# The first weight piece in an attention + squared-ReLU MLP kernel: its two exponent activations issued later on ScalarE, its three rounding instructions moved from the first pair of heads to the second

## The chip, the cores and the metric

The kernel runs on one core of a Trainium2 chip. The metric is the device time of one execution in microseconds (us). The kernel before has a median of 878.74 us in 4 runs (878.18 to 879.36).

## The reference

The reference is a hashed attention followed by a two-layer MLP. Cut to what matters:

```python
# attention: q, k, v are (4, 8, 768, 64) float32, proj is (64, 6)
q_bits = (einsum('bhsd,dk->bhsk', q, proj) > 0)      # k_bits the same from k
mask   = bucket(q_bits)[:, :, :, None] == bucket(k_bits)[:, :, None, :]
scores = where(mask, scale * q @ k.T, -1e9)
attn   = softmax(scores);  o = attn @ v
# MLP: x is o as (3072, 512); w_in (512, 2048) and w_out (2048, 512) are float64
h = x @ w_in;  g = maximum(h, 0) ** 2;  out = (g @ w_out).astype(float32)
```

The weights `w_in` and `w_out` come as float64, 8 bytes an element. The chip's engines work in float32 here, so the kernel rounds each weight to float32 itself, out of the two 32-bit halves of the float64.

## The kernel before, in words

The work has two stages. The first, up to about 331 us of the profiled span, is the attention. It goes over `NP` = 16 pairs of heads, `pr` = 0 to 15. The second is the MLP, in four chunks of 1024 tokens, with products cut by Strassen-like sums (lines 712 and 931 are its matmuls, lines 505 to 535 part of its sums).

**One pair of heads.** A pair has six key tiles `kt` = 0 to 5 of 128 keys each. Everything here is written out by hand in the loop over `pr`; each engine runs its instructions in the order of the program.

- `score(pr, kt)` (line 396) makes the scores of one key tile for all 768 queries of both heads, in two chunks: 512 queries (both heads together 128x1024) and 256 queries (128x512). Each chunk goes into a PSUM tile from `turn(...)`, a pool of three. After each chunk ScalarE (ACT) takes the exponential out of PSUM into one of four SBUF buffers (line 413). A fourth chunk can only be begun when the exponential of the chunk three before it has been read out of its PSUM tile.
- `add_up(pr, kt)` (lines 423 and 428) adds the exponentials on VectorE (DVE), and `attend(pr, kt)` (line 438) multiplies them with the values on TensorE (PE), into the one PSUM tile `xo`. `score` of two key tiles and `attend` of two others alternate.
- `features(pr + 1, w)` (line 333) transposes the queries and keys of the next pair on DVE. `hash_bits` (line 346) multiplies them with `proj` on PE, `signs` (line 356) takes eight sign activations on ACT, and `weigh` (line 382) scales the keys' bits with one activation.
- `finish(pr - 1)` runs inside pair `pr`, after `score(pr, 1)`: the next pair's hash, then the sums (`tot`, line 455), the last two `attend`, and `spread` (line 477), which needs the reciprocals `both` that DVE makes out of `tot` (lines 460, 462, 466). `normalize(pr - 1)` (lines 487 and 493) writes `x_t` out of `xo`. Only then is `xo` free for `attend(pr, 0)`.

In the text, "score (0,4)" is `score(0, 4)`: pair 0, key tile 4; its chunks are "first" (512 queries) and "second" (256 queries). "Pair 0" is the first pair, "pair 1" the second.

**The weights beside it.** There are 32 pieces of weight (128x512 elements), two in each pair: `a` = 2 pr and `b` = 2 pr + 1. Four steps make a piece:

- `load_weight(i)` (line 130) loads it on SyncE's (SP's) DMA queue into one of three buffers `raw`.
- `part_weight(i)` is two DVE instructions (lines 143 and 147) which take the exponent (`power`) and the fraction (`top`) out of it.
- `place_power(i)` is two ACT activations (line 160, a Relu into 8-bit `small`, and line 161, a Copy back into `power`), which shift the exponent's bias and put it where float32 has it.
- `round_weight(i)` is three DVE instructions (lines 171, 176 and 179). It needs `place_power(i)`, frees the `raw` buffer, and leaves the piece in `ins` (for `w_in`). For piece 0 it issues no DMA.

In each pair, piece `a` is parted before `score(pr, 2)`, its power placed after `score(pr, 3)`, and it is rounded after `add_up(pr, 3)`. Piece `b` is parted there, its power is placed after `score(pr, 5)`, and it is rounded in the next pair, behind `features`, as `round_weight(b - 2)`.

Pair 0 differs from the others in one thing that matters here: the eight `signs` for pair 1 are issued between `score(0, 2)` and `score(0, 3)`, and `weigh(1)` after `score(0, 5)`.

Of the kernel before, what the change touches and what calls it, by code (L numbers as in the profile page):

```python
# [34 lines left out]
def kernel(  # L35
# [68 lines left out]
    def turn(name):  # L104

        return ps_s.tile([P, 2, 512], FP32, name=name, tag="turn")
# [11 lines left out]
    def goal(i):  # L118
        if i < 2 * NIN:
            return ins[i // NIN][:, i % NIN // 2, i % 2]  # L120
        return p_t.tile([P, DM], FP32, name="out_piece", bufs=3)

    def load_weight(i):
        src, r, c = pieces[i]
        if src.dtype != U64:
            goals[i] = goal(i)
            nc.sync.dma_start(out=goals[i], in_=src[r:r + P, c:c + PIECE])
            return
        raw = p_w.tile([P, PIECE, 2], U32, name="raw", bufs=3)
        nc.sync.dma_start(  # L130
            out=raw.rearrange("p f w -> p (f w)"),
            in_=src.bitcast(U32)[r:r + P, 2 * c:2 * (c + PIECE)],
        )
        raws[i] = raw
# [18 lines left out]
    def place_power(i):  # L153


        if i not in parts:
            return
        power = parts[i][0]
        small = p_w.tile([P, PIECE], U8, name="small")
        nc.scalar.activation(out=small, in_=power, func=ACTF.Relu, bias=excess)  # L160
        nc.scalar.activation(out=power, in_=small, func=ACTF.Copy, scale=2.0**23)

    def round_weight(i):

        raw = raws.pop(i, None)
        if raw is None:
            return keep_weight(i)
        goals[i] = goal(i)
        low, high = raw[:, :, 0], raw[:, :, 1]
        power, top = parts.pop(i)  # L170
        nc.vector.scalar_tensor_tensor(
            out=power, in0=high, scalar=0x80000000, in1=power,
            op0=ALU.bitwise_and, op1=ALU.bitwise_or,
        )
        one = top.bitcast(FP32)
        nc.vector.scalar_tensor_tensor(
            out=one, in0=low, scalar=2.0**-32, in1=top, op0=ALU.mult, op1=ALU.add,
        )
        nc.vector.scalar_tensor_tensor(
            out=goals[i], in0=one, scalar=2.0**-20, in1=power.bitcast(FP32),  # L180
            op0=ALU.mult, op1=ALU.mult,
        )
        keep_weight(i)

    def keep_weight(i):

        t = goals.pop(i)
        j, c = divmod(i, NIN)
        if j >= 2:
            nc.sync.dma_start(out=w_out_1[:, i - 2 * NIN], in_=t)  # L190
        elif c == NIN - 1:
            nf = NFT // 2
            for n, f, h in (0, 0, 0), (1, nf, 0), (2, nf, 1):
                put_factor(n, j * PIECE, ins[j][:, f:f + nf, h])
            nc.sync.dma_start(
                out=w_in_21[:, :, j * PIECE:(j + 1) * PIECE], in_=ins[j][:, 0:nf, 1]
            )
# [81 lines left out]
    def load_pair(pr):  # L279


        b, j = divmod(pr, PB)
        for src, name in ((q, "q_nat"), (k, "k_nat")):
            t = p_qk.tile([P, S], FP32, name=name)
            for g in range(4):
                h, e = divmod(g, 2)
                nc.sync.dma_start(
                    out=t[g * 32:(g + 1) * 32].rearrange("i (c d) -> i c d", d=32),
                    in_=src[b, 2 * j + h].rearrange("(c i) (e d) -> e i c d", i=32, e=2)[e],
                )  # L290
            nat[pr, name] = t
# [38 lines left out]
    def features(pr, w):  # L330

        feat[pr, w] = p_f.tile([P, S], FP32, name=f"feat{w}")
        nc.vector.transpose(out=feat[pr, w], in_=nat[pr, ("q_nat", "k_nat")[w]])
# [3 lines left out]
    def hash_bits(pr, banks, ws=(0, 1), cs=(0, 1)):  # L337


        for w in ws:  # L340
            hashed[pr, w] = banks
            for c in cs:
                g = 2 * w + c
                for h in range(2):
                    rows = slice(h * D, (h + 1) * D)
                    nc.tensor.matmul(  # L346
                        out=banks[g * NR_B:(g + 1) * NR_B, h, 0:HS], lhsT=projs[rows],
                        rhs=feat[pr, w][rows, c * HS:(c + 1) * HS], start=True, stop=True,
                    )

    def signs(pr, w):
        bits[pr, w] = t = all_bits[pr % 2][w]
        for c in range(2):
            at = slice((2 * w + c) * NR_B, (2 * w + c + 1) * NR_B)
            for h in range(2):
                nc.scalar.activation(  # L356
                    out=t[h * D:h * D + NR_B, c * HS:(c + 1) * HS], in_=hashed[pr, w][at, h, 0:HS],
                    func=ACTF.Sign, scale=HUGE, bias=lifts[at],
                )
# [19 lines left out]
    def weigh(pr):  # L379

        t = bits[pr, 1]
        nc.scalar.activation(out=t, in_=t, func=ACTF.Copy, scale=gains)
# [139 lines left out]
    def sum_in(m):  # L522

        c, n = divmod(m, 4)
        j, h = divmod(c, 2)
        t, at = ins[j], slice(h * NS, (h + 1) * NS)
        nf = NFT // 2
        a11, a12, a21, a22 = (
            t[:, f:f + nf, g, at] for g in range(2) for f in (0, nf)
        )  # L530
        s = in_sums[m] = p_t.tile([P, nf, NS], FP32, name=f"s_in{n}", bufs=2)
        if n == 0:
            nc.vector.tensor_tensor(out=s, in0=a21, in1=a22, op=ALU.add)
        else:
            minus(s, *(
                (in_sums[4 * c], a11), (a11, a21), (a12, in_sums.get(4 * c + 1))
            )[n - 1])
        put_factor((3, 4, 5, 6)[n], c * NS, s)
# [12 lines left out]
    def load_x(i):  # L551

        x = p_c.tile([P, NFT, NCH], FP32, name="x")
        nc.gpsimd.dma_start(out=x, in_=x_all[:, :, i * NCH:(i + 1) * NCH])
        xs[i] = x, [p_c.tile([P, 2, NCH // 2], FP32, name=f"t_x{n}") for n in range(3)]
# [23 lines left out]
    def finish(pr, beside=None):  # L579

        tot = turn("tot")
        if beside:
            beside()
        sum_up(pr, tot)
        if pr == NP - 1:
            sum_x(0, 2)
            sum_x(0, 3)
        for kt in (SB - 2, SB - 1):
            attend(pr, kt)
        spread(pr)  # L590

    with tc.manual_schedule():
# [21 lines left out]
        for pr in range(NP):  # L614
            a, b = 2 * pr, 2 * pr + 1
            more = pr + 1 < NP

            def prepare():

                hash_bits(pr + 1, turn("hash"))  # L620
                for w in (1, 0):
                    signs(pr + 1, w)


            if pr + 2 < NP:
                load_pair(pr + 2)
            if pr == X_0:
                load_x(0)
            if more and pr > 0:
                for w in range(2):  # L630
                    features(pr + 1, w)
            if pr > 0:
                round_weight(b - 2)
                load_weight(b)
                for m in sums.get(pr, ()):
                    sum_in(m)
            score(pr, 0)
            if pr == 0:
                first_keys(1, turn("hash"))
            score(pr, 1)  # L640
            if pr == 0:
                for w in range(2):
                    features(1, w)
            if pr > 0:
                finish(pr - 1, prepare if more else None)
            add_up(pr, 1)
            if pr > 0:
                normalize(pr - 1)


            if pr == X_0 + 1:
                for n in range(2):
                    load_unit(n)
            part_weight(a)
            score(pr, 2)
            if pr == 0:
                prepare()
            score(pr, 3)
            if more and pr > 0:
                weigh(pr + 1)  # L660
            place_power(a)
            attend(pr, 0)
            attend(pr, 1)
            for kt in (2, 3):
                add_up(pr, kt)
            if more:
                load_values(pr + 1)


            round_weight(a)  # L670
            part_weight(b)
            if more:
                load_weight(a + 2)
            score(pr, 4)
            score(pr, 5)
            if pr == 0:
                weigh(1)
            place_power(b)
            attend(pr, 2)
            attend(pr, 3)  # L680
            add_up(pr, 4)
            add_up(pr, 5)
# [801 lines left out]
```

## Time and profile before

| | us |
|---|---|
| median of 4 runs | 878.74 (878.18 to 879.36) |
| the profiled execution's own time | 878.9 |
| its span (first to last instruction) | 877.1 |
| PE busy in the span | 864.9 (99%) |
| DVE busy | 759.9 (87%) |
| ACT busy | 391.5 (45%) |
| PE busy in 20 to 40 us / 40 to 60 us | 18.53 / 20.00 |
| DVE busy in 36 to 340 us (304 us) | 290.63 |

The granted TensorE clock is 1.00 in the attention stage (0.997 as a mean over the span).

A row of the timeline reads: start in us, length in us, engine, line, operation, output <- inputs, how many instructions are merged into the row, and in brackets how long the engine had been idle before it and what it was released by. A merged row's length is that of all its instructions; instructions on one engine can overlap a little, so that the distance from start to start is shorter than the length of one.

### The profile page before, as it was taken

To read this page: it belongs to the slowest core of one execution; us is meant where nothing else is said; L and a number is where in the kernel's file an instruction comes from. 1 tells how busy PE (TensorE), PEld (TensorE's weight loads), DVE (VectorE), ACT (ScalarE), POOL (GpSimd) and SP (SyncE) were. 2 spreads that over 40 slices of the span, in tenths; PEclk is the share of its full clock that TensorE was granted. 3 is DMA by queue.
4 is the path that set the end of the run, shared out by engine and by line. 5 is a ranking of instruction groups with operands and counts; after the bars stand their busy time and mean duration, and the time that the engine had idled before them with its cause. 6 is when DMAs were issued, how large, how long until landed. Compare 5 with 4: busy or idle time off the path is not lost.

```text
span 877.1 us, 12130 instructions
## 1 busy us (share of the span) xinstructions
PE 864.9 (99%) x4340; PEld 519.2 (59%) x4340; DVE 759.9 (87%) x1099; ACT 391.5 (45%) x673; POOL 107.0 (12%) x172
## 2 busy tenths in 40 slices
PE   8999999999999999999999999999999999999996
PEld 4444444444444444444688865556888755568885
DVE  5999999999999998888679978888889788888875
ACT  6988888888888852222211123332111233321110
POOL 2000000000000000554032021111000211110002
PEclk9999999999999999999999999999999999999998
DMA  9677977898888526999788774536856744355565
GB/s 177 145 147 133 224 166 151 188 252 226 179 178 224 165 98 211 299 268 284 298 285 274 207 167 166 174 119 221 283 155 183 167 165 156 124 167 154 158 173 106
DMA packets 224132, 167.09 MB, mean 190 GB/s; under 512 B 164449, under 2 KB 181345, under 8 KB 224065
## 3 DMA queue, kind: packets, MB, share of 16 engines
q1 hardware_dynamic: 189152, 87.19, 41.0%
q0 software_dynamic: 12528, 41.30, 15.2%
q10 hardware_dynamic: 22384, 37.76, 14.1%
q8 instruction: 36, 0.59, 0.3%
q14 instruction: 32, 0.25, 0.1%
HBM read 124.52 MB, written 41.68 MB: 189 GB/s over the span
## 4 chain that ended last, share of the span: by engine, by line
PE 96%; DVE 2%; ACT 1%; DMA 1%; issue 0%; ACTq 0%; DVEq 0%
PE acc L712 40%; PE st L396 17%; PE acc L931 16%; PE xo L438 14%; PE acc L884 6%; PE hash L346 2%; PE tot L455 1%; DVE total L428 1%; DMA k_nat<-in_k_dram 1%; ACT bits L356 1%; ACT e L413 0%; PE xo L477 0%; DVE x_t L493 0%; PE tp L309 0%; DVE recs L487 0%
## 5 line engine op out<-in xcount | busy, mean ns | idle before, releaser
L413 ACT ACTIVATE e<-st 128x1024 f32<-128x1024 f32 x192 | 145.1, 810 | 44.9 <-PE st L396 41.0
L396 PE MATMUL st<-feat,feat 64*128 64x512 f32 (+1 forms) x768 | 150.4, 483 | 0.0
L438 PE MATMUL xo<-e,v_nat 128*64 128x512 f32 (+1 forms) x768 | 134.8, 492 | 0.0
L712 PE MATMUL acc<-b,leaf 128*128 128x256 f32 x600 | 133.2, 379 | 0.3 <-issue 0.3
L712 PEld LDWEIGHTS acc<-b,leaf 128*128 128x128 f32 x600 | 113.8, 190 | 16.6 <-issue 1.3
L428 DVE TENSOR_TENSOR total<-total,e 128x1536 f32<-128x1536 f32 x64 | 112.4, 1757 | 8.2 <-ACT e L413 3.6
L438 PEld LDWEIGHTS xo<-e,v_nat 128*64 128x64 f32 x768 | 51.3, 136 | 82.1 <-issue 74.3
L931 PE MATMUL acc<-t_x,w_unit 128*128 128x512 f32 x192 | 90.2, 592 | 0.0
L396 PEld LDWEIGHTS st<-feat,feat 64*128 64x128 f32 x768 | 66.0, 188 | 33.0 <-issue 23.2
L712 PE MATMUL acc<-t,leaf 128*128 128x256 f32 x336 | 76.2, 380 | 0.0
L356 ACT ACTIVATE bits<-hash,lifts 32x384 bf16<-32x384 f32 x120 | 68.6, 572 | 2.3 <-PE hash L346 0.5
L712 PEld LDWEIGHTS acc<-t,leaf 128*128 128x128 f32 x336 | 63.7, 190 | 9.1 <-DVE t L516 0.5
L796 DVE SCALAR_TENSOR_TENSOR b<-h 128x512 f32<-128x512 f32 x96 | 65.7, 691 | 3.0
L396 PE MATMUL st<-bits,bits 64*128 64x256 bf16 (+1 forms) x384 | 63.1, 325 | 1.7 <-ACT e L413 1.2
L931 PE MATMUL acc<-x,w_unit 128*128 128x512 f32 x128 | 60.1, 592 | 0.0
L712 PE MATMUL acc<-x,w_unit 128*128 128x512 f32 x128 | 56.6, 594 | 0.0
L712 PE MATMUL acc<-b_t,leaf 128*128 128x256 f32 x240 | 53.8, 379 | 0.0
L931 PEld LDWEIGHTS acc<-t_x,w_unit 128*128 128x128 f32 x192 | 36.5, 190 | 28.9 <-issue 26.8
L719 ACT COPY two<-acc 128x256 f32<-128x256 f32 (+1 forms) x29 | 12.5, 431 | 87.8 <-PE acc L712 81.5
L719 ACT COPY one<-acc 128x256 f32<-128x256 f32 (+1 forms) x29 | 12.5, 431 | 84.7 <-PE acc L712 60.9
L712 PEld LDWEIGHTS acc<-b_t,leaf 128*128 128x128 f32 x240 | 45.5, 190 | 6.2
L396 PEld LDWEIGHTS <-bits 64*128 64x128 bf16 x384 | 23.5, 93 | 42.5 <-issue 38.4
(159 smaller groups left out, 1165.9 us busy)
## 6 DMA issues: line engine op xcount, KB each, us to landing
leaf<-w_out ACTq DMA_DIRECT2D x142, 256.0 KB, 3.1
w_unit<-w_in SPq DMA_DIRECT2D x16, 640.0 KB, 4.0
raw<-in_moe_w_in_dram SPq DMA_DIRECT2D x16, 512.0 KB, 5.5
raw<-in_moe_w_out_dram SPq DMA_DIRECT2D x16, 512.0 KB, 4.3
w_unit<-w_in SPq DMA_DIRECT2D x8, 896.0 KB, 8.2
w_out<-sums POOLq DMA_DIRECT2D x16, 448.0 KB, 6.8
sum<-w_in SPq DMA_DIRECT2D x16, 448.0 KB, 4.9
v_nat<-in_v_dram SPq DMA_DIRECT2D x16, 384.0 KB, 4.3
```

The lines of the kernel that those rows point to most:

```text
L346: nc.tensor.matmul(out=banks[g * NR_B:(g + 1) * NR_B, h, 0:HS], lhsT=projs[rows], rhs=feat[pr, w][rows, c * HS:(c + 1) * HS], start=True, ...
L356: nc.scalar.activation(out=t[h * D:h * D + NR_B, c * HS:(c + 1) * HS], in_=hashed[pr, w][at, h, 0:HS], func=ACTF.Sign, scale=HUGE, bias=li ...
L396: nc.tensor.matmul(out=st[:, h, 0:hi - lo], lhsT=src[pr, 1][rows, key], rhs=src[pr, 0][rows, lo:hi], start=first, stop=not first,)
L413: nc.scalar.activation(out=e[:, :, lo:hi], in_=sts[i][:, :, 0:hi - lo], func=ACTF.Exp, scale=scale)
L428: nc.vector.tensor_tensor(out=totals[pr], in0=totals[pr], in1=weights[pr, kt][:, :, 0:S], op=ALU.add)
L438: nc.tensor.matmul(out=xo[h * D:(h + 1) * D, lo:hi], lhsT=nat[pr, "v_nat"][:, h, kt * D:(kt + 1) * D], rhs=weights[pr, kt][:, h, lo:hi], s ...
L455: nc.tensor.matmul(out=tot[g * 32:(g + 1) * 32, 0:HS], lhsT=ones, rhs=totals[pr][:, h, c * HS:(c + 1) * HS], start=True, stop=True,)
L712: nc.tensor.matmul(out=acc[to], lhsT=a(i), rhs=b(i), start=first and i == 0, stop=last and i == n - 1, skip_group_check=True,)
L719: nc.scalar.copy(out=t, in_=acc[of])
L796: nc.vector.scalar_tensor_tensor(out=out, in0=h, scalar=0.0, in1=h, op0=ALU.max, op1=ALU.mult)
L884: nc.tensor.matmul(out=out, lhsT=w[:, a], rhs=b, start=start, stop=stop, skip_group_check=True)
L931: nc.tensor.matmul(out=acc[to], lhsT=w[:, PLACE[a], f], rhs=bt[b](f), start=first and f == 0, stop=last and f == NFT // 2 - 1, skip_group_ ...
```

## The change

Three calls are moved, all of weight piece 0 (`a` in pair 0); the work stays the same.

- `place_power(0)`: two ACT activations, from after `score(0, 3)` to after `weigh(1)`, that is behind the four exponentials of `score(0, 4)` and `score(0, 5)`, and ahead of `place_power(1)`.
- `round_weight(0)`: three DVE instructions, from after `add_up(0, 3)` in pair 0 to pair 1, behind `features(2, ...)` and ahead of `round_weight(1)`.

`part_weight(0)` stays where it is. On DVE, `part_weight(1)` now follows `add_up(0, 3)` directly. In pairs 1 to 15 nothing else changes.

```diff
             if pr > 0:
+                if pr == 1:
+                    round_weight(0)
                 round_weight(b - 2)
                 load_weight(b)
...
             if more and pr > 0:
                 weigh(pr + 1)
-            place_power(a)
+            if pr > 0:
+                place_power(a)
             attend(pr, 0)
...
-            round_weight(a)
+            if pr > 0:
+                round_weight(a)
             part_weight(b)
...
             if pr == 0:
                 weigh(1)
+                place_power(0)
             place_power(b)
```

## The prediction

> **What bounds the kernel now.** I read three views: the page's chain, the same chain piece by piece in the first 42 us, then each engine's timeline there. The page, first:
>
> ```profile
> PE 96%; DVE 2%; ACT 1%; DMA 1%; issue 0%; ACTq 0%; DVEq 0%
> ```
>
> PE sets the end almost everywhere, so time can be won only where PE stands still. The waits of PE name few such places after 36 us: one of 0.4 us at 327.44, and in the MLP 0.8 and 0.3 us. The chain by pieces shows where ACT holds the end instead, in pair 0:
>
> ```profile
> 21.28 1.51 ACT e L413 x2
> 22.79 0.03 issue
> 22.82 0.73 ACT small L160
> 23.55 0.02 issue
> 23.57 0.63 ACT power L161
> 24.20 0.92 ACT e L413
> 25.12 0.04 issue
> 25.16 0.72 PE st L396 x6
> ```
>
> The two activations that the change moves are links of the chain: the exponential of score (0,4)'s first chunk stands behind them, and PE's fourth chunk, score (0,5)'s second, waits for it. PE's and DVE's rows, then ACT's:
>
> ```profile
> 25.16 0.29 PE L396 MATMUL st<-bits,bits 64*128 64x256 bf16 x2 [0.99 <-ACT e L413]
> ...
> 31.89 1.47 PE L346 MATMUL hash<-feat,projs 64*32 64x384 f32 x16
> ```
>
> ```profile
> 24.50 0.69 DVE L171 SCALAR_TENSOR_TENSOR power<-raw,power 128x512 uint32<-128x512 uint32 x1
> ...
> 30.63 0.97 DVE L333 STREAM_TRANSPOSE feat<-q_nat 128x768 f32<-128x768 f32 x1
> 31.53 0.94 DVE L333 STREAM_TRANSPOSE feat<-k_nat 128x768 f32<-128x768 f32 x1
> ...
> 38.13 1.02 DVE L493 SCALAR_TENSOR_TENSOR x_t<-xo,recs 128x768 f32<-128x768 f32 x1
> ```
>
> ```profile
> 26.87 0.95 ACT L382 ACTIVATE bits<-bits,gains 128x768 bf16<-128x768 bf16 x1
> 27.69 0.74 ACT L160 ACTIVATE small<-power,excess 128x512 uint8<-128x512 uint32 x1
> 28.46 0.63 ACT L161 ACTIVATE power<-small 128x512 uint32<-128x512 uint8 x1
> 29.85 3.13 ACT L413 ACTIVATE e<-st 128x1024 f32<-128x1024 f32 x4 [0.76 <-PE st L396]
> ```
>
> The reader is to see PE's 0.99 us gap; a hash of 1.47 us, where that of pair 2 takes 0.88 us (PE's weight loads wait 0.47 us for `feat`); and a DVE that has work without a break from 22.82 to the end of `x_t` at 39.15.
>
> **Step 1, the gap in pair 0.** Without the two activations the exponential of (0,4)'s first chunk starts at about 22.82, where line 160 did; its score is ready since 22.56. It lasts 1.02 us, to 23.84. PE begins (0,5)'s first chunk at 22.92 and is 1.08 us later (21.30 to 22.38 in the row before) at the next, 24.00: the PSUM tile is free then. So (0,5)'s second chunk goes from 25.16 to 24.00: **-1.16 us** on PE. The two `attend` behind it have had their inputs since 22.79, so score (1,0) goes from 28.56 to 27.40.
>
> **Step 2, the two activations in their new place.** ACT's distances from start to start in the timeline: first exponential 0.90, second 0.48, `weigh` 0.82, line 160 0.77, line 161 0.54. From 22.82: (0,4) takes 22.82 and 23.72; (0,5)'s first waits for its score until 24.20, its second starts at 25.10; `weigh(1)` at 25.58 (it was 26.87); then line 160 and 161 of piece 0 at 26.40 and 27.17, those of piece 1 at 27.71 and 28.48, end 29.11. (The exponent that piece 1 needs is there: on DVE its parting moves from 26.43 to 24.50.) The next exponential, of score (1,0), could have its score 1.29 us after PE starts it (28.56 to 29.85 now), at 28.69, and gets ACT at about 29.02. It is held 0.33 us. Who waits for it: PE's fourth chunk of pair 1, (1,1)'s second, which needs its end, 29.02 + 1.03 + 0.04 = 30.09; PE arrives there at 31.26 - 1.16 = 30.10. The cover is used up to 0.01 us; cost nothing. Should ACT be 0.4 us later, the next steps show a slack of 0.44 us that takes it.
>
> **Step 3, DVE between.** Three rounding instructions leave 24.50 to 26.43: everything up to `features(2)` is 1.93 us earlier. The sums of (0,4) and (0,5) would start at 25.17 and 26.93, behind their exponentials (24.3 and 25.7), so DVE has no new wait. `features(2)` run at 28.70 and 29.60, end 30.54; their inputs were issued by 20.10 and land in at most 8.3 us (all line 287's rows). PE comes to the hash at 31.89 - 1.16 = 30.73, finds both halves, and needs 0.88 instead of 1.47 us: **-0.59 us** more, -1.75 in all when it comes to `tot` (33.30, now 31.55; the PSUM tile it waits for, by ACT's steps of above, is free at 31.46).
>
> **Step 4, where it is given back.** DVE then rounds two pieces instead of one ahead of `flip`: 30.46 + 1.93 + 2.01 (32.39 to 34.40) = 34.40. That is where `flip` is now: the three instructions have only changed sides with work that also had to be done. `both` ends at 35.53 as now. PE's last two `attend` of pair 0 end at 36.89 - 1.75 = 35.14, and `spread` waits for `both` until 35.58: +0.44. After it and score (1,2), (1,3), PE comes to attend (1,0) at 40.24 - 1.31 = 38.93, which needs `xo`, so the end of `x_t`: 39.15, plus 0.05. It starts at 39.20, not 40.24. DVE, not PE, sets this point, and DVE's work up to it is unchanged. Sum: -1.16 - 0.59 + 0.44 + 0.27 = **-1.04 us**.
>
> **Step 5, the rest.** From there PE is 1.04 us early and DVE not. DVE catches up where it waits for PE or ACT: 0.23 us at 43.60 (for ACT's `power`, which comes earlier too), and
>
> ```profile
> 54.12 0.58 DVE L460 STREAM_TRANSPOSE flip<-tot 128x384 f32<-128x384 f32 x1 [0.65 <-PE tot L455]
> ...
> 74.03 0.58 DVE L460 STREAM_TRANSPOSE flip<-tot 128x384 f32<-128x384 f32 x1 [0.65 <-PE tot L455]
> ```
>
> By 74 us it can have gained 0.23 + 0.65 + 0.65 = 1.53, more than 1.04, so both engines are shifted alike; the one later wait of PE for DVE (0.4 us at 327.44) shifts with them. On the way the tightest point is the hash of pair 3, at 52.40 - 1.04 = 51.36: its second half needs `features` by 51.80, and they end at 51.57 at the latest. On SP, the load of piece 3 (29.05 now) waits for `raw` of piece 0 until its second rounding step, about 31.7; the next transfer behind it is the store of `x_t`, 39.18, and piece 3 is parted only at 45.54. It costs nothing; without that cover it would cost at most its 2.7 us of delay. Nothing else is issued by the moved calls.
>
> **A rule weighed.** The whole trace has one ACT_TABLE_LOAD, of 1283 ns at 2.59 us; between the exponentials and the Relu and Copy of lines 160 and 161 there is 0.03 us. The Trainium skill, "ScalarE: Activation LUTs", section "What ACT_TABLE_LOAD costs", puts about 2.66 us on every switch to another set of functions. If these were switches, grouping the exponents would save two of them, an estimate of some 5 us; the same page's section "Table sets: the hidden batching unit" has relu and copy in every set, by which grouping saves nothing of the kind. The rows side with the second.
>
> **Sum.** The profiled execution took 878.9 us (span 877.1); 878.9 - 1.04 = 877.86. The median of the runs shown is 878.74, 0.16 below that execution; I forecast **877.7 us** for the median. That is 0.12% faster, and 0.2% (1.76 us) is about what a measurement of this kernel can tell from no change.
>
> **Rivals.**
> - *More.* If DVE does not hold PE at `spread` and attend (1,0), the whole -1.75 us stays: 877.0. For it: step 3's two stalls are both seen in the rows. Against it: DVE is busy 15.95 of the 16.35 us from 22.80 to 39.15. Chance 0.12.
> - *Nothing.* One row speaks for it: the weight loads of score (1,0) have idle time put down to ACT's line 160 of piece 1 ("PEld L396 <- ACT small L160", 0.4 us), not to `weigh`. If PE really waits for the activation behind `weigh`, it waits until 28.5 again (that activation still ends at 28.45), score (1,0) starts at 28.56, and nothing is won: 878.7. Against it: `attend` ended at 28.56, so PE was not free earlier. Chance 0.13.
> - *Slower.* DVE's first rounding in pair 1 waits for ACT's `power` of piece 0, and behind it stand the second rounding, `flip`, `both` and `x_t`. By step 2 `power` is there at 27.80, and DVE comes at 30.46. If it came after 31.5, `x_t` would end after 40.19 and attend (1,0) be later than before. That takes an ACT that runs the exponentials of pair 1 ahead of it (they end at 33): rounding at about 34.3, 2.8 us beyond the deciding point: 881.5. ACT's order as written is against it. Chance 0.05.
>
> **Numbers.** Forecast 0.70. Range 876.9 to 879.0: the first rival below, the second above, each with about a tenth of a per cent at most for the spread of the runs (878.18 to 879.36). Faster by over 0.2% (below 876.98) has half of the first rival and the forecast's tail, 0.10; slower 0.05; within 0.2% 0.85.
>
> **What would show it.** Step 1: line 396 at 24.0 without a wait for `e`. Step 2: line 160 twice in a row behind `weigh`, and the four exponentials of pair 1 starting at about 29.0 without idle time before them. Step 3: a hash of 0.88 us at 30.7. Step 4: `flip` at 34.4 as before, a wait of PE for DVE ahead of line 477, and attend (1,0) at 39.2. Step 5: `tot` of pair 15 at 326.4, and the span 1.0 us shorter. An attend (1,0) earlier than 39.0 or later than 39.5 would make me wrong at step 4; a span that doesn't follow it, at step 5.

## The result, and the profile after

The changed kernel has a median of 877.44 us (876.78 to 878.36, 40 runs); the kernel before, in 60 runs, 878.55 us. The ratio is 0.9987, with a 95% interval of [0.9983, 0.9991]: 1.11 us faster, where -1.04 was forecast. A second comparison on one chip gave 877.56 to 878.69 us, ratio 0.9989 [0.998, 0.9998].

The chain by pieces, in the first 42 us of the changed kernel:

```profile
21.26 3.41 PE st L396 x24
24.67 2.74 PE xo L438 x16
27.41 1.21 PE st L396 x6
28.62 0.06 issue
28.67 1.83 DVE feat L333 x2
30.50 0.57 DVE power L171
...
34.36 0.59 DVE flip L460
...
35.31 0.20 DVE both L466
35.51 0.04 issue
35.55 0.30 PE xo L477 x4
35.85 3.34 PE st L396 x24
39.20 2.78 PE xo L438 x16
```

The two activations are no link of it any more: PE makes the scores of (0,4) and (0,5) in one go, 3.41 us without a gap. From 28.7 to 35.5 us the chain runs over DVE, through both roundings, `flip` and `both`, and comes back to PE at line 477. That is step 4 of the prediction. ACT's timeline, behind the last six exponentials of pair 0:

```profile
25.76 0.94 ACT L382 ACTIVATE bits<-bits,gains 128x768 bf16<-128x768 bf16 x1
26.60 0.71 ACT L160 ACTIVATE small<-power,excess 128x512 uint8<-128x512 uint32 x1
27.34 0.63 ACT L161 ACTIVATE power<-small 128x512 uint32<-128x512 uint8 x1
27.88 0.71 ACT L160 ACTIVATE small<-power,excess 128x512 uint8<-128x512 uint32 x1
28.62 0.63 ACT L161 ACTIVATE power<-small 128x512 uint32<-128x512 uint8 x1
29.15 2.89 ACT L413 ACTIVATE e<-st 128x1024 f32<-128x1024 f32 x4
```

PE's timeline:

```profile
30.21 0.28 PE L396 MATMUL st<-bits,bits 64*128 64x256 bf16 x2
...
30.86 0.88 PE L346 MATMUL hash<-feat,projs 64*32 64x384 f32 x16
...
35.55 0.30 PE L477 MATMUL xo<-both,picks 128*64 128x24 f32 x4 [0.30 <-DVE both L466]
...
39.17 2.81 PE L438 MATMUL xo<-e,v_nat 128*64 128x512 f32 x16
...
326.37 0.85 PE L455 MATMUL tot<-total,ones 128*32 128x384 f32 x8 [0.43 <-DVE total L428]
```

DVE's `x_t` of pair 0 in the changed kernel, and PE's rows of the kernel before at the same places:

```profile
38.09 1.02 DVE L493 SCALAR_TENSOR_TENSOR x_t<-xo,recs 128x768 f32<-128x768 f32 x1
```

```profile
36.72 0.25 PE L477 MATMUL xo<-both,picks 128*64 128x24 f32 x4
...
40.24 2.81 PE L438 MATMUL xo<-e,v_nat 128*64 128x512 f32 x16
...
327.44 0.85 PE L455 MATMUL tot<-total,ones 128*32 128x384 f32 x8 [0.42 <-DVE total L428]
```

The reader is to see four things. The hash is down to 0.88 us. There is a new wait of 0.30 us for `both`. Attend (1,0) starts at 39.17, right behind the end of `x_t` (38.09 + 1.02 = 39.11). And `tot` of pair 15, 287 us later, is early by the same amount (326.37, before 327.44).

Executions differ by up to half a microsecond in their first 20 us, so traces are compared below from the start of score (0,4), which no kernel here moves: 21.30 before, 21.26 in the changed one. The table gives attend (1,0) and `tot` of pair 15 from there, and their difference to the kernel before.

| kernel | attend (1,0) | `tot` of pair 15 | median against before in the same comparison |
|---|---|---|---|
| before | 18.94 | 306.14 | |
| changed | 17.91 (-1.03) | 305.11 (-1.03) | 0.9987 [0.9983, 0.9991] |
| e1 | 18.94 (0.00) | 306.15 (+0.01) | 1.0001 [0.9992, 1.0011] |
| e2 | 18.70 (-0.24) | 305.91 (-0.23) | 0.9994 [0.9985, 1.0003] |
| e3 | 17.36 (-1.58) | 305.29 (-0.85) | 0.9986 [0.9977, 0.9995] |
| e4 | 17.16 (-1.78) | 304.37 (-1.77) | 0.9981 [0.9972, 0.999] |
| e5 | 20.09 (+1.15) | 307.29 (+1.15) | 1.0028 [1.0017, 1.0039] |
| e6 | 20.08 (+1.14) | 307.29 (+1.15) | 1.0011 [1.0002, 1.002] |
| e7 | 24.14 (+5.20) | 311.35 (+5.21) | 1.0048 [1.0035, 1.0062] |
| e8 | 17.36 (-1.58) | 304.56 (-1.58) | 0.9977 [0.9968, 0.9986] |
| r1 (changed again) | 17.92 (-1.02) | 305.12 (-1.02) | 0.9989 [0.998, 0.9998] |
| r2 (e8 again) | 17.35 (-1.59) | 304.55 (-1.59) | 0.998 [0.9971, 0.9989] |

One per mille is 0.88 us. The intervals of single comparisons are about as wide as the effects; the traces separate the kernels where the medians don't.

The spans of the two profiled executions differ by 1.6 us (877.1 and 875.5), 0.6 more than `tot` of pair 15 does. Before's execution has a gap of 0.28 us in the MLP, at 474.57, with no releaser in the profile, which the other has not; the rest of the 0.6 us was not traced. The medians do not have it.

### The profile page after: what moved, and what is told of

It reads as the page before. It is cut to its first block, busy times and chain, and to the rows that moved or that the text cites. A ratio compares the mean times of both kernels' runs of the same rounds, so it can differ in the third digit from the quotient of the medians.

```text
span 875.5 us, 12135 instructions
## 1 busy us (share of the span) xinstructions
PE 864.3 (99%) x4340; PEld 519.2 (59%) x4340; DVE 759.9 (87%) x1099; ACT 391.5 (45%) x673; POOL 107.1 (12%) x172
## 4 chain that ended last, share of the span: by engine, by line
PE 96%; DVE 2%; ACT 1%; issue 0%; DVEq 0%; ACTq 0%
PE acc L717 40%; PE st L396 17%; PE acc L936 16%; PE xo L438 14%; PE acc L889 6%; PE hash L346 1%; PE tot L455 1%; DVE total L428 1%; ACT bits L356 0%; PE xo L326 0%; PE tp L309 0%; DVE power L171 0%; DVE top L176 0%; DVE feat L333 0%; PE xo L477 0%
```

## The experiments

**e1: the exponents without the rounding.** The kernel before, with this edit:

```diff
-            place_power(a)
+            if pr > 0:
+                place_power(a)
...
             if pr == 0:
                 weigh(1)
+                place_power(0)
             place_power(b)
```

> The kernel before (878.55 us) with only the two exponent activations moved; the three rounding instructions of piece 0 stay in pair 0. Theory (DVE's order sets what is kept): on DVE the rounding stands ahead of the sums of (0,4) and waits for the activations that now come behind weigh, from 24.5 to about 28.0, so DVE loses 3.5 us; features(2) start at about 34.1, hash of pair 2 ends at 36.5, attend (1,0) starts at about 43.4 instead of 40.24. Time 881.7 (881.0 to 882.3). Rival (the stall of PE in pair 0 is all that matters, DVE has slack): 1.16 us faster, 877.4.

It is not the kernel that I described. `round_weight(0)` stands ahead of the new `place_power(0)` in the program, and takes piece 0 out of the list that `place_power` looks in, so that nothing is placed: the two activations are left out altogether, and piece 0 is rounded with the exponent as it came. My 881.7 us says nothing about it. As it stands it is a sharper test of the rival named with it: ACT is cleared of the two activations at no price, and DVE's order is that of the kernel before. PE's and DVE's timelines:

```profile
24.59 2.81 PE L438 MATMUL xo<-e,v_nat 128*64 128x512 f32 x16
...
31.70 1.62 PE L346 MATMUL hash<-feat,projs 64*32 64x384 f32 x16 [0.96 <-DVE feat L333]
...
40.19 2.81 PE L438 MATMUL xo<-e,v_nat 128*64 128x512 f32 x16
```

```profile
30.58 0.97 DVE L333 STREAM_TRANSPOSE feat<-q_nat 128x768 f32<-128x768 f32 x1
31.48 0.93 DVE L333 STREAM_TRANSPOSE feat<-k_nat 128x768 f32<-128x768 f32 x1
```

PE comes to `attend` 1.18 us earlier (24.59 against 25.82, less 0.05 for the start), and stands 0.96 us ahead of the hash instead, waiting for `features(2)`. Nothing is won at all. The rival is out: the gap of pair 0 was on the chain, and taking it away alone gives nothing, because DVE's features are late next.

e1 also settles the rival "nothing", in which PE waits for the activation behind `weigh`. ACT's row and PE's row:

```profile
26.83 0.72 ACT L160 ACTIVATE small<-power,excess 128x512 uint8<-128x512 uint32 x1
```

```profile
27.33 0.39 PE L396 MATMUL st<-bits,bits 64*128 64x512 bf16 x2
```

Score (1,0) starts at 27.33, while that activation runs until 27.55.

**e2: the rounding without the exponents.** The kernel before, with

```diff
             if pr > 0:
+                if pr == 1:
+                    round_weight(0)
                 round_weight(b - 2)
...
-            round_weight(a)
+            if pr > 0:
+                round_weight(a)
```

> The kernel before with only the three rounding instructions moved to pair 1; the exponents stay. Theory: PE's 0.99 us gap ahead of score (0,5)'s second chunk stays, the hash of pair 2 at 31.89 takes 0.88 instead of 1.47 us, and PE comes to spread at 36.3, after both (35.53), so all 0.59 us is kept: attend (1,0) at 39.65, time 878.0 (877.7 to 878.2). Rival (the gain is the gap of pair 0 alone): no change, 878.55. Rival (rounding ahead of flip costs what it saves): 878.55 too, with a wait at spread.

The hash takes 0.88 us, as expected, but only 0.24 us is left at attend (1,0). PE's and ACT's timelines:

```profile
32.33 0.88 PE L346 MATMUL hash<-feat,projs 64*32 64x384 f32 x16
...
36.74 0.39 PE L396 MATMUL st<-bits,bits 64*128 64x512 bf16 x2
36.97 1.02 PE L396 MATMUL st<-feat,feat 64*128 64x512 f32 x4
38.18 0.29 PE L396 MATMUL st<-bits,bits 64*128 64x256 bf16 x2 [0.19 <-ACT bits L356]
```

```profile
33.45 4.68 ACT L356 ACTIVATE bits<-hash,lifts 32x384 bf16<-32x384 f32 x8
```

Score (1,2)'s second chunk comes 1.44 us after its first instead of 1.08: it waits until the eight `signs` are through (33.45 + 4.68 = 38.13). That is 0.36 us of the 0.59. In the kernel before the same chunk starts ahead of the end of the signs (37.99 and 38.12). The waits of the built programs say why: in the kernel before this chunk waits for PE and (1,3)'s first for ACT; in e2 and in the changed kernel it is the other way round. The pool of three PSUM tiles has handed the hash's tile to another chunk, though no line about it was edited. So e2 does not have the rounding alone, and both of its rivals fell with the theory's size: by the trace something is won, and less than 0.59 (the medians alone, 0.9994 [0.9985, 1.0003], would not show it). In the changed kernel the signs end at 32.07 + 4.68 = 36.75 and this chunk starts at 36.87: the swap costs nothing there, by 0.12 us. In every kernel here but e2 the chunk comes 1.08 or 1.09 us after the first.

**e3: the rounding behind `x_t`.** The changed kernel, with

```diff
             if pr > 0:
-                if pr == 1:
-                    round_weight(0)
                 round_weight(b - 2)
-                load_weight(b)
+                if pr > 1:
+                    load_weight(b)
...
                 normalize(pr - 1)
+            if pr == 1:
+                round_weight(0)
+                load_weight(b)
```

> The changed kernel (877.44 us) with the rounding of piece 0, and the load of piece 3 that needs its buffer, moved on behind x_t of pair 0 in pair 1. Theory (DVE holds PE at spread and at attend (1,0) in the changed kernel): flip at 32.6 instead of 34.36, no wait at spread, attend (1,0) at 38.6 instead of 39.17; then DVE is behind, and the second half of the hash of pair 3 waits about 0.2 us for features. Against before -1.43 us, time 877.1 (876.8 to 877.3). Rival (DVE does not hold PE there): 877.44, attend (1,0) at 39.2.

Attend (1,0) is 1.58 us earlier than before, 0.55 earlier than in the changed kernel, and there is no wait at line 477: DVE had held PE there. But 0.73 of the 1.58 us is lost again, nearly all of it one pair later. The hash of pair 3, and below it its second eight passes alone:

```profile
51.00 1.59 PE L346 MATMUL hash<-feat,projs 64*32 64x384 f32 x16
...
51.75 0.85 PE L346 MATMUL hash<-feat,projs 64*32 64x384 f32 x8
```

The hash of pair 3 takes 0.71 us longer than the 0.88 of a free one, not the 0.2 I expected. `features(3)` end at 50.76 + 0.94 = 51.70, and the second half, alone, takes nearly as long as both halves together (see the last section). At `tot` of pair 15 e3 is 0.85 us ahead of before, and 0.18 behind the changed kernel. Moving DVE's work past one waiter put it in front of the next.

**e4: piece 0 dropped.** The changed kernel without `place_power(0)` and `round_weight(0)`; GpSimd sets that part of `ins` to zero at the start, so that the output lacks one piece of `w_in`.

```diff
-                    round_weight(0)
+                    parts.pop(0), raws.pop(0)
...
-                place_power(0)
...
         constants()
+        nc.gpsimd.memset(goal(0), 0.0)
```

> The changed kernel without the two exponent activations and the three rounding instructions of piece 0 (its goal is set to zero by GpSimd once: this part of w_in is left out). It bounds what any place for these five instructions can give. Theory: -1.16 and -0.59 us are both kept, attend (1,0) at 38.5, no wait of PE for DVE or ACT up to pair 4: -1.75 us against before, time 876.8 (876.5 to 877.1). Rival (a later wait takes back what comes early): 877.4 as the changed kernel.

-1.78 us at attend (1,0) and -1.77 at `tot` of pair 15: the two stalls are worth the 1.75 us of steps 1 and 3, and nothing later takes any of it back. As long as nothing else is changed, it is the bound for every place of these five instructions.

**e5 and e6: three more DVE instructions ahead of `flip`,** in the changed kernel (e5) and in the kernel before (e6):

```diff
-        nc.vector.scalar_tensor_tensor(
-            out=goals[i], in0=one, scalar=2.0**-20, in1=power.bitcast(FP32),
-            op0=ALU.mult, op1=ALU.mult,
-        )
+        for _ in range(4 if i == 1 else 1):
+            nc.vector.scalar_tensor_tensor(
+                out=goals[i], in0=one, scalar=2.0**-20, in1=power.bitcast(FP32),
+                op0=ALU.mult, op1=ALU.mult,
+            )
```

> The changed kernel with the last rounding instruction of piece 1 issued four times instead of once in pair 1, ahead of flip (the same result each time): three more DVE instructions of some 0.62 us, 1.9 us. Theory (in the changed kernel DVE sets spread and attend (1,0)): every bit of it counts, attend (1,0) at 41.1 instead of 39.17, 1.9 us slower than the changed kernel, and so as slow as the kernel before with the same three instructions: 0.8 to 0.9 us above before. Rival (PE sets them, DVE has about 1 us of room): 0.9 us slower than the changed kernel at most, about 0.2 us under before.

> The kernel before with the same three DVE instructions at the same place. Theory: x_t ends 1.04 us before PE comes to attend (1,0) in the kernel before, so the first 1.04 us is covered and the rest, 0.85 us, counts: attend (1,0) at 41.1, 0.85 us above before, the same as the changed kernel with them. Rival (DVE has no bearing on PE here): no change; rival (DVE sets PE in the kernel before too): 1.9 us slower.

PE's timelines, e5 first and then e6:

```profile
37.70 0.30 PE L478 MATMUL xo<-both,picks 128*64 128x24 f32 x4 [2.47 <-DVE both L467]
...
41.32 2.81 PE L439 MATMUL xo<-e,v_nat 128*64 128x512 f32 x16
...
328.52 0.85 PE L456 MATMUL tot<-total,ones 128*32 128x384 f32 x8 [0.42 <-DVE total L429]
```

```profile
41.34 2.81 PE L439 MATMUL xo<-e,v_nat 128*64 128x512 f32 x16
...
328.55 0.85 PE L456 MATMUL tot<-total,ones 128*32 128x384 f32 x8 [0.42 <-DVE total L429]
```

The two kernels, 1.03 us apart without the extra work, are equal with it. Each of the instructions takes 0.72 us from start to start (34.34, 35.07, 35.79 in e5's chain), together 2.18 and not 1.9. In the changed kernel all of it counts (-1.03 to +1.15); in the kernel before the first 1.04 is covered (2.18 - 1.04 = 1.14). This is the slack of step 4, measured from both sides. e5's median is 1.6 us above e6's all the same, and the clock goes with it: in three of its eight executions the mean granted clock was 0.997 and the times 879.53 to 880.42 us, in five it was 0.994 to 0.996 and the times 881.32 to 882.53. Its profiled execution is one of the first (879.71 us).

**e7: the rounding right behind the moved exponents, in pair 0.** The changed kernel, with

```diff
             if pr > 0:
-                if pr == 1:
-                    round_weight(0)
                 round_weight(b - 2)
...
             if pr == 0:
                 weigh(1)
                 place_power(0)
+                round_weight(0)
```

> The changed kernel with the rounding of piece 0 directly behind its moved exponents in pair 0, ahead of the sums of (0,4), instead of in pair 1. Theory: DVE waits from 25.2 to 28.0 for the exponent, the sums and features(2) come 2.8 us later than in the kernel before, the hash of pair 2 ends at about 36.2 (its second half alone takes 0.85 us, as e3's rows show), attend (1,0) at 43.1: 2.9 us above before (2.4 to 3.2). Rival (taking the exponents out of PE's way is what counts): 1 us below before.

This is what e1 was to show. DVE's row, PE's rows, and PE's stretches, first of 4 us, then of 0.5 us (from and to, length, busy time and count, granted clock, DMA share, GB/s):

```profile
28.13 0.69 DVE L171 SCALAR_TENSOR_TENSOR power<-raw,power 128x512 uint32<-128x512 uint32 x1 [2.77 <-ACT power L161]
```

```profile
34.65 2.27 PE L346 MATMUL hash<-feat,projs 64*32 64x384 f32 x16 [3.59 <-DVE feat L333]
36.85 1.51 PE L455 MATMUL tot<-total,ones 128*32 128x384 f32 x8
38.29 3.90 PE L438 MATMUL xo<-e,v_nat 128*64 128x512 f32 x16
```

```profile
32.00:36.00 4.00, 1.35 (x12) 0.71 0.19 77
36.00:40.00 4.00, 4.00 (x24) 0.50 0.02 4
40.00:44.00 4.00, 4.00 (x32) 0.93 0.00 0
```

```profile
33.00:33.50 0.50, 0.00 (x0) 1.00 0.10 33
33.50:34.00 0.50, 0.00 (x0) 0.70 0.00 0
...
40.50:41.00 0.50, 0.50 (x6) 0.98 0.00 0
```

DVE's wait of 2.77 us came as expected (2.8), the price did not: 5.2 us at attend (1,0) instead of 2.9. In PE's wait of 3.59 us the granted clock fell to 0.50, where it stayed until about 40.5, and hash, `tot` and `attend` took 2.27, 1.51 and 3.90 us. From the start of the hash to line 477 that is 7.36 us (34.65 to 42.01); e1, whose second half of the hash comes late too but whose PE waits only 0.96 us, needs 4.96 (31.70 to 36.66). These 2.40 us account for the 2.3 between 2.9 and 5.2. The sign of the theory held, the size had left out the clock. The rival (1 us faster) is out: the exponents can only be moved because the rounding is moved farther.

**e8: the rounding spread over three pairs.** The changed kernel, with the three instructions of `round_weight(0)` one each behind `normalize` in pairs 1, 2 and 3 (`round_step(n)` issues the n-th), and tiles of its own for piece 0, since it now keeps them for three pairs:

```diff
-                if pr == 1:
-                    round_weight(0)
...
                 normalize(pr - 1)
+            if 0 < pr < 4:
+                round_step(pr - 1)
...
-        raw = p_w.tile([P, PIECE, 2], U32, name="raw", bufs=3)
+        raw = p_w.tile([P, PIECE, 2], U32, name="raw" if i else "raw0", bufs=3 if i else 1)
...
```

> The changed kernel with the three rounding instructions of piece 0 one each behind x_t in pairs 1, 2 and 3 (piece 0 has tiles of its own for it), where DVE waits 0.65 us for tot in pairs 2 and 3 when piece 0 is dropped. Theory: nothing of it reaches PE; as with piece 0 dropped, but for the 0.1 us that ACT holds the fourth score chunk of pair 1: 1.6 to 1.7 us below before, 0.5 to 0.6 below the changed kernel. Rival (each DVE instruction ahead of the next features costs PE): 1.1 us below before or less.

DVE's timeline shows where the work went:

```profile
33.07 0.58 DVE L483 STREAM_TRANSPOSE flip<-tot 128x384 f32<-128x384 f32 x1 [0.19 <-PE tot L478]
...
37.85 0.68 DVE L191 SCALAR_TENSOR_TENSOR power<-raw,power 128x512 uint32<-128x512 uint32 x1
...
52.98 0.58 DVE L483 STREAM_TRANSPOSE flip<-tot 128x384 f32<-128x384 f32 x1 [0.47 <-PE tot L478]
```

`flip` waits for PE again, in pair 1 and, with one instruction more ahead of it, still in pair 2. -1.58 us at attend (1,0) and at the end of the stage: 0.2 us short of e4. In this kernel the fourth score chunk of pair 1 still waits for ACT, as in the changed one: it comes 1.25 us behind the third (29.45 and 30.70) instead of 1.08, which is 0.17 of the 0.2. The time is 876.83 us, ratio 0.9977 [0.9968, 0.9986].

**r1 and r2: the changed kernel and e8 once more, on one chip.**

> The changed kernel as it is, beside r2 and the kernel before on one chip. Theory: 1.0 to 1.1 us below before, attend (1,0) 17.9 us after the start of score (0,4), where it is 18.94 before.

> The kernel with the rounding of piece 0 spread over pairs 1 to 3 once more, for a comparison with the changed kernel on one chip. Theory: attend (1,0) 17.36 us after the start of score (0,4), 1.58 us earlier than before, and nothing given back: 1.5 to 1.8 us below before, 0.5 us below the changed kernel. Rival: no difference from the changed kernel, and the 2.0 us of the first comparison was scatter.

877.56 and 876.93 us, with the kernel before at 878.69. The traces repeat to 0.01 us. e8 is the fastest kernel of this case that computes all of it, by 0.6 us over the changed one; the 2.0 us of its first comparison was too much by scatter, while the 0.6 stands in the traces as well (17.92 against 17.35).

## Why the prediction was right

- *Step 1, -1.16 us.* Shown: the gap is gone, and `attend` starts 1.18 us earlier (24.60 - 21.26 against 25.82 - 21.30). e1 shows that it is worth nothing by itself, e4 that it is worth its full size with the rest.
- *Step 2, nothing, with 0.01 us of cover.* The order on ACT was as written, but `weigh` started at 25.76, not 25.58, and the first exponential of pair 1 at 29.15, not 29.02. PE's fourth chunk came at 30.21 instead of 30.05 (1.08 behind the third, 28.97): 0.16 us, not 0. From (0,5)'s second exponential to `weigh` it was 0.62 us from start to start (25.14 to 25.76) instead of the 0.48 that step 2 took; why is open. The 0.16 was taken by the slack that step 2 named. In e8, where DVE no longer holds PE, it counts: the kernel is 0.2 us short of e4.
- *Step 3, -0.59 us.* Shown: the hash takes 0.88 us, and `tot` comes 1.59 us earlier; with the 0.16 of step 2 this is the 1.75.
- *Step 4, +0.44 and +0.27.* The sum and its cause are shown, the split is not. This is the step on which the forecast turned. `flip` stands at 34.36 as worked out, PE waits 0.30 us at line 477, and attend (1,0) follows the end of `x_t`. But the step set `spread`'s start against 36.89, the end of `attend`'s row; `spread`'s own row starts at 36.72 in the kernel before. So `spread` was to be held not by 0.44 but by 0.61 us, and attend (1,0) by another 0.10 instead of 0.27. Measured, with the 0.16 of step 2 already spent: 0.46 at `spread` (from 1.59 us early at `tot` to 1.13, 14.29 against 15.42 from the start of score (0,4)) and 0.10 at attend (1,0). Neither slip moves the sum, because the end of `x_t` alone sets it. e5 and e6 show it from the other side. The rival "more" named its condition rightly: at attend (1,0), e4, e8 and e3, where DVE does not hold PE there, are 1.78, 1.58 and 1.58 us early.
- *Step 5, no further loss.* Shown: -1.03 at attend (1,0) and at `tot` of pair 15, and -1.11 in the medians. The span, named as a sign, fell by 1.6 us instead of 1.0; the 0.6 more is in the MLP of single executions. One term was wrong and was not put to the test by the change: the step let `features` of pair 3 end up to 0.44 us behind the start of the hash (51.36 and 51.80) at no cost. e3, where they end 0.70 us behind it, pays 0.71 us, so there is no such cover. In the changed kernel they end at 51.19 (50.26 + 0.93), ahead of the hash at 51.33.
- *The sum.* 877.7 was forecast, 877.44 measured. Of the 0.26 us between them, 0.19 is the median of the kernel before, 878.74 in the 4 runs that the forecast started from and 878.55 in 60.
- The rival "nothing" is out: score (1,0) starts at 27.34 while ACT's line 160 of piece 1 starts only at 27.88. What stands directly behind `weigh` now is line 160 of piece 0, and it ends at 27.31, just ahead of the score; but PE does not wait for it either. In e1 the score does not wait for the activation there, and from `attend` to score (1,0) it is 2.74 us from start to start before, in the changed kernel and in e1 alike. The rival "slower" is out: `power` of piece 0 was ready at 27.97, 2.5 us ahead of DVE's rounding at 30.43.

What the prediction did not see, and what would have cost it had it fallen otherwise: the exchange of two PSUM tiles in pair 1 that e2 brought to light.

## What to carry to other kernels

When a stall is taken off the chain, work out at once which engine is late next, and up to which instruction its own order is unchanged: here DVE's list up to `x_t` was the same length before and after, so its end set what is left of the gain (1.04 of 1.75 us were forecast, 1.03 measured). Work that may be done at any time did best here when it was cut into single instructions and laid where its engine waits soon after (e8); in one block it only chose which waiter it delayed (e1, the changed kernel, e3, e7). And after an edit compare the waits of the built program, not only its order: a tile pool may hand out its buffers differently though nothing about it was edited (e2).

## What the runs showed of the hardware

- **Half a hash costs nearly as much as a whole one.** With the features of both queries and keys at hand the 16 matmul passes take 0.88 us (30.86). When the second eight come late, they take 0.85 us alone: before from 32.52, and in e3 from 51.75. So the two halves, side by side, take hardly longer than one. They write to different 32-partition groups of the output; that this is the reason is argued, not shown. A hash with a late half ends 0.85 us after that half starts: in the kernel before, 0.63 us behind the first half and 1.47 us in all; in e3, 0.75 us behind it and 1.59 in all, so that e3 lost 0.71 us where 0.2 was expected.
- **A long wait of PE halves its clock for a while; here the clock fell 2.6 us into it.** In e7 PE's last matmul ahead of the wait ends at 31.06 (30.45 + 0.61). The granted clock is 1.00 up to 33.5 and 0.50 from 34.0, with a mean of 0.70 between, so it fell at about 33.7, some 2.6 us into the wait of 3.59. It came back at about 40.5; that added 2.4 us against e1's rows. All five executions of e7 have a mean clock of 0.993 to 0.995, against 0.996 to 0.998 in the executions of the kernel before. The Trainium skill, "TensorE: Matmul & The Clock Gate", section "Part 1: The HAM clock gate", puts the step to half rate after an idle window of about 3.4 us. By e7 it comes sooner than that after the last matmul. In e5 a wait of 2.47 us was followed by a mean clock of 0.994 to 0.996 in five of eight executions; the profiled one is not among them (1.00 in all its stretches from 20 to 48 us), so that it was the same step at the same place is argued, not shown.
